# The gated MLP's products and the weighted sums as pairs of 64-row products that change banks halfway, in a sparse attention with a gated MLP

## The chip, the cores and the metric

The kernel runs on one core of a Trainium2 chip. The metric is device time in microseconds (us); lower is better. A profiled execution has a time of its own and a span, the stretch that the profile covers.

## The reference

Inputs are fp32: q, k, v of 4 batches, 8 heads, 768 tokens and 64 dimensions, and the weights of a gated MLP. Attention looks only at the six best of the causal blocks ("chunks") of 32 keys, which are ranked by an upper bound of their scores.

```python
k_min, k_max = min and max of k over each chunk of 32 keys
ub = sum_d maximum(q * k_min, q * k_max)              # bound, causal chunks only
sel = the 6 chunks of highest ub per query
scores = where(sel and key <= query, q @ k.T / 8, -1e9)
x = softmax(scores) @ v                                # heads side by side: [4, 768, 512]
h = relu(x @ w_in)                                     # [4, 768, 1024]
u, v = h[..., :512], h[..., 512:]
v_n = (v - mean(v)) / sqrt(var(v) + 1e-6)
v_s = w_spatial @ v_n + b_spatial                      # mixes tokens
out = (u * v_s) @ w_out                                # [4, 768, 512]
```

## The kernel before

Two heads make a pair `p` (16 in all, four to a batch): their 64 dimensions fill partitions 0 to 63 and 64 to 127. Each pair runs through the same pieces: q, k and v are loaded by SP's queue, cast to fp16 (`cast`), and q and k are turned, by TensorE (`turn`) for pairs 0 to 4 and by a DMA for the others. DVE takes the extremes of each chunk (`ext`, L671). TensorE makes the bounds (`bounds`, L702), DVE finds the sixth best (`top`, `leave`). TensorE makes all causal scores (`pk`, L732, L735 and L786) of which DVE takes the highest per chunk (`mx`, L795 to L807); for the first three pairs (`FOLD = 3`) the scores are first folded in two with a relu on ACT (`fd`, `fr`, `fi`, `fb`, L748 to L766). GpSimd and DVE join both into a bias (`minus`, `kept`, `shift`), TensorE turns it (`turn_bias`, L831). Scores are then made a second time with keys on the partitions, plus the bias (`probs`, L856 and L863), ACT takes exponents (`ex`, L871), GpSimd cuts above the diagonal (`cut`), TensorE makes the weighted sums of v (`weigh`, L885; one piece per head, 21 products of 65 columns), ACT copies them, and GpSimd or DVE normalises (`norm`, L907).

The MLP runs once per batch: `hv` (L937, six pieces of 512 columns), relu (`vr`), mean and variance (`bn`, `rstd`), `vn`; `hu` (L990, eight pieces of 384) with relu (`uT`); `mix` (L1001, eight pieces of six products of 384) is the token mixing; the spatial bias `bB` is added by GpSimd or DVE (`plus`, L1010 and L1012), `gT` (L1019) multiplies by u, and `og` (L1024, six pieces of four products of 512) gives the output, which ACT or DVE copies (`oe`) and SP's queue stores (`od`).

Scores, bounds, `turn_bias` and `fd`/`fb` use products on 64 rows of TensorE: the two heads' products stand next to each other in the program, one on rows 0 to 63, one on 64 to 127, with outputs in different PSUM banks. The weighted sums, the MLP and the turns use all 128 rows. PSUM is divided in three two-bank slots (`two`) for the former and two single banks (`mg`) for the latter; the last batch's MLP uses both.

The order of all pieces is written out: `RANK` gives each piece its rank, `WHERE` the engine where there is a choice, and `Work.order()` runs through time with the cost of each piece (`on`), gives every engine the ready piece of lowest rank, and assigns buffer slots. It reckons 0.095 us where TensorE changes between `TILED` pieces and others:

```python
if e == "PE" and tiled != (name[0] in self.TILED):
    tiled, took = not tiled, took + 0.095
```

The engines then carry out their lists strictly in that order, SP its DMA issues too.

## Time and profile before

| | |
|---|---|
| time, median of 3 runs | 248.54 us (248.27 to 248.81) |
| profiled execution: its own time, its span | 248.22 us, 246.5 us |
| ACT exponents (L871) | 96 instructions, 85.3 us busy |
| DVE peaks (L807) | 104 instructions, 85.3 us busy |
| PE weighted sums (L885) | 672 products, 25.9 us busy |
| PE token mixing (L1001) | 192 products, 30.2 us busy for the 168 in the single banks |
| granted TensorE clock | 1.00 |

A row of the page's list of groups reads: line, engine, operation, output<-inputs, rows*columns of the array or partitions x elements, count | busy time, mean ns of one | idle time just before, and what ended it. PE is TensorE's products, PEld its weight loads, DVE VectorE, ACT ScalarE, POOL GpSimd, SP SyncE. A product's duration reaches from its start until its last result is out, so the products of a run overlap. The profile's timeline gives the start, the length until the last one's end and the count of equal instructions that follow each other.

### The profile page before, as it was taken

The page shows a single profiled execution, that of the slowest core. Times are in us where ns is not written, and L with a number is a line of the kernel's source. Part 1 is how long each engine was busy: PE and PEld are TensorE (multiplying, and loading weights), DVE is VectorE, ACT ScalarE, POOL GpSimd, SP SyncE. Part 2 cuts the span into 40 slices and gives each one's busy share as a digit, 9 for nine tenths or more (in the row PEclk, how much of TensorE's full clock was granted, in tenths as well). Part 3 has the DMA queues.
Part 4 walks back from the last instruction along what each step waited for, and adds up shares of the span by engine and source line. Part 5 has one row for each costly group of instructions (what it writes and reads, how often), then busy time and mean ns, then how long its engine had stood idle before and what let it go on. Part 6 is the DMA issues. An engine that isn't in the chain of part 4 may idle for free.

```text
span 246.5 us, 9019 instructions
## 1 busy us (share of the span) xinstructions
PE 224.9 (91%) x3780; PEld 144.6 (59%) x3780; DVE 206.5 (84%) x512; ACT 191.9 (78%) x298; POOL 165.9 (67%) x209
## 2 busy tenths in 40 slices
PE   0898778878999999999999999999999999999993
PEld 0656457666755675666665576666745566645551
DVE  4799999999999999799998997899998853349670
ACT  3598887979998999587859897897679969767312
POOL 8879749887785377999965929999926147402160
PEclk9999999999999999999999999999999999999999
DMA  7969996699999949484899997128900010350005
GB/s 189 325 186 201 257 242 127 122 164 241 168 186 235 216 82 187 89 170 112 190 161 271 175 200 125 34 75 140 268 22 19 0 36 0 105 188 0 0 28 227
DMA packets 93895, 35.51 MB, mean 144 GB/s; under 512 B 86208, under 2 KB 90144, under 8 KB 93856
## 3 DMA queue, kind: packets, MB, share of 16 engines
q1 hardware_dynamic: 91568, 31.81, 61.9%
q0 software_dynamic: 2016, 2.75, 6.5%
q8 instruction: 29, 0.48, 0.8%
q10 hardware_dynamic: 272, 0.39, 0.5%
q14 instruction: 10, 0.08, 0.1%
HBM read 24.77 MB, written 6.29 MB: 126 GB/s over the span
## 4 chain that ended last, share of the span: by engine, by line
PE 48%; DVE 28%; ACT 14%; DMA 4%; issue 3%; POOL 2%; DVEq 0%; ACTq 0%
DVE cmax L807 11%; PE mg L1001 11%; ACT pr L871 8%; PE mg L1024 6%; PE mg L885 5%; PE two L856 4%; PE mg L937 3%; PE two L863 3%; DVE stats L954 3%; DVE ext L671 3%; PE two L786 3%; DVE top L715 2%; PE mg L990 2%; DMA k<-in_k_dram 2%; DVE cmax L801 2%
## 5 line engine op out<-in xcount | busy, mean ns | idle before, releaser
L871 ACT ACTIVATE pr<-two 128x1024 f16<-128x1024 f32 (+1 forms) x96 | 85.3, 934 | 5.4 <-PE two L863 4.8
L807 DVE TENSOR_REDUCE cmax<-two 128x24 f32<-128x768 f32 (+4 forms) x104 | 85.3, 843 | 3.5 <-PE two L735 2.0
L856 PE MATMUL two<-qT,kT 64*128 64x128 f16 (+3 forms) x384 | 40.5, 258 | 5.4 <-ACT bT L835 1.9
L863 PE MATMUL two<-bT,member 64*128 64x128 f16 (+1 forms) x512 | 39.7, 233 | 0.0
L877 POOL TENSOR_SCALAR_AFFINE_SELECT pr<-pr 128x768 f16<-128x768 f16 x32 | 27.9, 886 | 9.1 <-ACT pr L871 9.0
L1019 POOL TENSOR_TENSOR vr<-tmp,uT 128x384 f16<-128x384 f32 x27 | 24.5, 922 | 11.9 <-DVE tmp L1012 11.8
L671 DVE TENSOR_REDUCE ext<-kT 128x24 f16<-128x768 f16 x32 | 29.5, 936 | 1.9 <-ACT kT L617 1.7
L1001 PE MATMUL mg<-wsT,vn 128*128 128x384 f16 x168 | 30.2, 327 | 0.0
L856 PEld LDWEIGHTS <-kT 64*128 64x128 f16 x384 | 19.9, 94 | 17.2 <-issue 15.1
L863 PEld LDWEIGHTS <-member 64*128 64x128 f16 x512 | 25.7, 94 | 5.1
L885 PE MATMUL mg<-v,pr 128*128 128x65 f16 x672 | 25.9, 194 | 0.7 <-POOL pr L877 0.5
L786 PE MATMUL two<-kT,qT 64*128 64x384 f16 (+4 forms) x182 | 24.6, 280 | 1.4 <-ACT pr L871 0.5
L885 PEld LDWEIGHTS <-pr 128*128 128x128 f16 x672 | 23.1, 98 | 3.6 <-issue 1.0
L1001 PEld LDWEIGHTS <-vn 128*128 128x128 f16 x192 | 17.7, 98 | 12.2 <-issue 0.6
L990 PE MATMUL mg<-xT,w_in_sb 128*128 128x384 f16 x112 | 22.4, 328 | 0.0
L907 POOL TENSOR_TENSOR x<-av,rc 128x768 f16<-128x768 f32 x11 | 16.2, 1469 | 8.8 <-DVE rc L900 4.9
L732 PE MATMUL two<-kT,qT 64*128 64x128 f16 x192 | 19.6, 221 | 2.3 <-ACT qT L617 1.0
L1024 PE MATMUL mg<-w_out_sb,vr 128*128 128x512 f16 x84 | 20.8, 380 | 0.0
L937 PE MATMUL mg<-w_in_sb,xT 128*128 128x512 f16 x84 | 20.3, 380 | 0.4 <-DVE o L619 0.4
L889 ACT COPY av<-mg 128x390 f32<-128x390 f32 x32 | 15.6, 500 | 6.2 <-PE mg L885 6.0
L954 DVE BATCH_NORM_STATS2 stats<-vr 128x6 f32<-128x512 f32 x24 | 16.6, 692 | 4.0 <-ACT vr L942 2.9
L735 PE MATMUL two<-half_ahead,ident 64*128 64x64 f16 x192 | 19.8, 193 | 0.0
(113 smaller groups left out, 496.8 us busy)
## 6 DMA issues: line engine op xcount, KB each, us to landing
q<-in_q_dram SPq DMA_DIRECT2D x16, 384.0 KB, 6.4
v<-in_v_dram SPq DMA_DIRECT2D x16, 384.0 KB, 5.7
out_dram<-o SPq DMA_DIRECT2D x24, 256.0 KB, 2.1
k<-in_k_dram SPq DMA_DIRECT2D x15, 384.0 KB, 5.7
vr<-in_moe_w_spatial_dram POOLq DMA_DIRECT2D x6, 192.0 KB, 5.6
w_in_sb<-in_moe_w_in_dram POOLq DMA_DIRECT2D x4, 256.0 KB, 8.8
w_out_sb<-in_moe_w_out_dram POOLq DMA_DIRECT2D x4, 128.0 KB, 4.5
k<-in_k_dram ACTq DMA_DIRECT2D x1, 384.0 KB, 4.7
```

Of the source, the lines that this page charges most:

```text
L671: nc.vector.tensor_reduce(held["ext", p][:, m], src, axis=AX.X, op=Alu.min if m else Alu.max, negate=(m == 1))
L786: mm(t[:, h, o:o + before], lhsT=qT[rows[h], c], rhs=kT[rows[h], a * CH:a * CH + before], start=True, stop=True)
L807: nc.vector.tensor_reduce(tops(p)[:, i // 2, :, i % 2, a:z], held["two", (p, u)][:, :, o:o + n].rearrange("p h (c e) -> p h c e", e=CH), a ...
L856: mm(t[:, h, z:z + n * P], lhsT=kT[rows[h], keys], rhs=qT[rows[h], i * P:(i + n) * P], start=True, stop=False)
L863: mm(d, lhsT=member[rows[h], r, keys], rhs=bT[rows[h], m * P:(m + w_) * P].rearrange("c (m s) -> c m s", s=P), start=False, stop=(n == 1 o ...
L871: nc.scalar.activation(out=held["pr", p][:, :, c0:c0 + n], in_=held["two", (p, "e", c0)][:, :, 0:n], func=Act.Exp, scale=scale)
L877: nc.gpsimd.affine_select(out=d, in_=d, compare_op=Alu.is_ge, fill=0.0, base=0, channel_multiplier=-1, pattern=[[0, NT], [1, P]])
L885: mm(a[:, i, :], lhsT=pr[:, at[t, i]:at[t, i] + P], rhs=vp[:, h * NT + t, :], start=(t == 0), stop=(t == i))
L937: mm(t, lhsT=held["xT", b][:, ko, i * P:(i + 1) * P], rhs=w_in_sb[:, ko, DH:2 * DH], start=(ko == 0), stop=(ko == NDO - 1))
L990: mm(t, lhsT=w_in_sb[:, ko, db * P:(db + 1) * P], rhs=held["xT", b][:, ko, s * HS:(s + 1) * HS], start=(ko == 0), stop=(ko == NDO - 1))
L1001: mm(t, lhsT=held["vn", b][:, si, db * P:(db + 1) * P], rhs=wsT[:, si, s * HS:(s + 1) * HS], start=(si == 0), stop=(si == NT - 1))
L1024: mm(t, lhsT=held["vr", ("g", b)][:, ko, i * P:(i + 1) * P], rhs=w_out_sb[:, ko, :], start=(ko == 0), stop=(ko == KO - 1))
```

## The change

- `weigh` and the MLP's products of batches 0 to 2 become 64-row pairs. A piece now fills two banks (two heads, two token tiles, or two halves of the columns). In the first round the pair's products use the lower 64 rows for bank 0 and the upper 64 for bank 1, in the second round (`weigh2`, `hv2`, `hu2`, `mix2`, `og2`) the other way round. Between them stands a `relay`: an empty instruction on SP that waits for the first round's last product, and for which the second round's first product waits. There are 58 relays.
- One PSUM ring of four two-bank slots serves everything; evictions of the MLP and of `av` are twice as wide and half as many.
- The spatial bias is added by TensorE: `b_parts` makes two fp16 parts of it, and products with `pick` start each `mix` piece with it. `plus` goes. For batches 2 and 3 DVE's `gT` reads PSUM.
- `FOLD` goes from 3 to 5, other peaks are cut in blocks of 768 and 1024 columns; the causal mask of the bounds is always TensorE's (`EARLY = 16`), so ACT or DVE only copies them.
- The first k comes in two halves; `warm` puts ten products at the start. Casts and `less` may run on ACT, `vn` on GpSimd.
- `RANK` and `WHERE` are new. The last batch's MLP stays on 128 rows.

```diff
-    DELAY = {"PE": 0.25, "DVE": 0.17, "ACT": 0.18, "POOL": 0.14, "SP": 0.0}
-    TILED = ("pk", "probs", "bounds", "turn_bias", "fd", "fb")
+    DELAY = {"PE": 0.25, "DVE": 0.17, "ACT": 0.18, "POOL": 0.14, "SP": 0.15}
+    TILED = ("pk", "probs", "bounds", "turn_bias", "fd", "fb", "weigh", "weigh2", "hv2", "hu2", "mix2", "og2")
+    SPLIT = ("hv", "hu", "mix", "og")
...
-UNITS = [((0, 0, 4), (1, 0, 8)), ((2, 0, 12),), ((3, 0, 16),), ((4, 0, 10),), ((4, 10, 20),), ((5, 0, 12),), ((5, 12, 24),)]
-PEAKS = [(u, i, a, z) for u, segs in enumerate(UNITS) for i, a, z in segs]
+STEPS = ((1, 0, 4), (3, 8, 12), (5, 16, 20))
+UNITS = [STEPS] + [((2 * m, c, c + 8), (2 * m + 1, c, c + 8)) for m, c in ((1, 0), (2, 0), (2, 8))]
+FOLDS = [((4, 0, 16), (5, 0, 16)), ((2, 0, 8), (3, 0, 8)) + STEPS]
+FOLDED = ((0, FOLDS[0]), (1, FOLDS[1][:2]), (1, STEPS))
...
-EARLY = 6
-FOLD = 3
-FOLDS = [(5, 3), (4, 2, 1)]
+EARLY = 16
+FOLD = 5
...
+WARM = (7, 2, 1)
...
-PLUS_POOL = 2
+GATE_POOL = 2
...
-                  cmax=2, kept=2, less=2, av=2, tmp=4, qT=4, rc=2, bias=2, bT=3, kd=2, fr=2, pr=2, x=8, xT=2, vr=1, vn=1, uT=1, o=5, two=3, mg=2))
+                  cmax=2, kept=2, less=2, av=2, tmp=3, qT=4, rc=2, bias=2, bT=3, kd=2, fr=2, pr=2, x=8, xT=2, vr=1, vn=1, uT=1, o=3, two=4))
...
+    for x, n in enumerate(WARM):
+        w.add(("warm", x), {"PE": 0.427 * n}, -9 + 4 * x, after=[(("spark",), ("turn", 0, "k", 1), ("turn", 0, "q"))[x]], new=[("two", ("warm", x))])
...
+            if (p, nm) == (0, "k"):
+                for x in range(2):
+                    add("load", {"SP": 0.46} if x else {"ACT": 0.5}, DUE["load_k"] - 1, nm, x, new=[] if x else [("k32", 0)], old=[("k32", 0)] if x else [], dma=(1.1, 0.4)[x])
+                    add("cast", {"DVE": dve(S // 2, 0.52), "ACT": act(S // 2)}, DUE["cast"], nm, x, after=[("load", 0, nm, x)], new=[] if x else [("k16", 0)],
+                        old=[("k32", 0)] + [("k16", 0)] * x)
+                continue
...
-            add("cast", {"POOL": pool(S)} if p else {"DVE": dve(S, 0.52)} if nm == "k" else {"ACT": act(S)}, DUE["cast"] + 0.05 * (nm == "q"), nm,
+            add("cast", {"POOL": pool(S), "ACT": act(S)} if p else {"DVE": dve(S, 0.52)} if nm == "k" else {"ACT": act(S)}, DUE["cast"] + 0.05 * (nm == "q"), nm,
...
-            add("minus", {"POOL": 0.55}, DUE["leave"] + 0.01, after=[("leave", p)], old=[("bias", p)], new=[("less", p)])
+            add("minus", {"POOL": 0.55, "ACT": 0.35}, DUE["leave"] + 0.01, after=[("leave", p)], old=[("bias", p)], new=[("less", p)])
...
+        at, src = DUE["weigh"], ("two", ("av", p))
+        add("weigh", {"PE": NT * (NT + 1) / 2 * 0.0322}, at, after=[("cut", p, h) for h in range(2) if p >= CUT_PE] + [("cast", p, "v")] + ex,
+            old=[("pr", p), ("v16", p)], new=[src])
+        w.add(("relay", "av", p), {"SP": 0.1}, p + at, after=[("weigh", p)])
+        add("weigh2", {"PE": NT * (NT + 1) / 2 * 0.0322}, at, after=[("relay", "av", p)], old=[("pr", p), ("v16", p), src])
+        add("av", {"ACT": act(2 * NT * (D + 1))}, at, after=[("weigh2", p), ("small",)], old=[src], new=[("av", p)])
+        add("sum", {"DVE": 0.12}, at, after=[("av", p)], old=[("av", p)], new=[("rc", p)])
+        add("inv", {"DVE": 0.14}, at, after=[("sum", p)], old=[("rc", p)])
+        add("norm", {"POOL": 1.5, "DVE": 1.15}, at, after=[("inv", p)], old=[("av", p), ("rc", p)], new=[("x", p)])
...
+        def relay(kind, n, *args):
+            w.add(("relay", kind, b) + args, {"SP": 0.1}, HP * b + DUE["gmlp"] + n * DUE["gmlp_step"], after=[(kind, b) + args])
+
+        def group(n, make, pe, args, need, old, done, on, tag, first):
+            buf = ("two", (make, b) + args)
+            if not last:
+                add(make, {"PE": pe / 2}, n, *args, after=need, old=old, new=[buf])
+                relay(make, n, *args)
+                make += "2"
+                add(make, {"PE": pe / 2}, n, *args, after=[("relay", make[:-1], b) + args], old=old + [buf])
+            else:
+                add(make, {"PE": pe}, n, *args, after=need, old=old, new=[buf])
+            add(done, on, n, *args, after=[(make, b) + args],
+                old=[buf] + ([] if first else [(tag, b)]), new=[(tag, b)] if first else [])
...
-                add("vn", {"ACT": 0.705, "DVE": 0.47} if last else {"ACT": 0.705}, NT + i, i, after=[("rstd2", b, g)], old=[("vr", b)] + ([("vn", b)] if i else []),
+                add("vn", {"ACT": 0.705, "DVE": 0.5} if last else {"ACT": 0.705, "POOL": 0.75}, NT + i, i, after=[("rstd2", b, g)], old=[("vr", b)] + ([("vn", b)] if i else []),
...
+            add("mix", {"PE": (NT + 1) * col(HS)}, NT + 8 + m, *part, after=need, old=[("vn", b)], new=[buf])
+            if not last:
+                relay("mix", NT + 8 + m, *part)
+                add("mix2", {"PE": NT * col(HS)}, NT + 8 + m, *part, after=[("relay", "mix", b) + part], old=[("vn", b), buf])
...
+            if b >= GATE_POOL:
+                add("gT", {"DVE": 0.15 + each * 0.4}, NT + 8 + m, *part, after=[mixed, ("uT", b) + part], old=[buf, ("uT", b)] + [g] * (m > 0), new=[] if m else [g])
+                continue
+            add("ms", {"ACT": act(each * HS)}, NT + 8 + m, *part, after=[mixed], old=[buf], new=[t])
+            for x in range(2):
+                add("gT", {"POOL": 0.92, "DVE": 0.7}, NT + 8 + m, *part, x, after=[("ms", b) + part, ("uT", b) + part],
...
+    def k_b_parts(e, x):
+        if x == 0:
+            nc.gpsimd.tensor_copy(b_row, b_raw)
+            for n, t in enumerate(pick):
+                nc.gpsimd.memset(t, 0.0)
+                for g in range(4 >> n):
+                    nc.gpsimd.memset(t[g * CH:g * CH + 1], 1.0 / (2048.0 if g % 2 else 1.0))
+            return
+        r = slice(D * x - CH, D * x)
+        nc.gpsimd.tensor_sub(b_raw[r], b_raw[r], b_row[r])
+        nc.gpsimd.tensor_scalar(b_row[r], in0=b_raw[r], scalar1=2048.0, scalar2=1.0, op0=Alu.mult, op1=Alu.mult)
...
-            each = [(big, far[:, i])] * (p < EARLY) + [(qT[:, c], x[:, 0]), (qp[:, c], x[:, 0]), (qp[:, c], x[:, 1])]
+            each = [(big, far[:, i])] + [(qT[:, c], x[:, 0]), (qp[:, c], x[:, 0]), (qp[:, c], x[:, 1])] * (i > 0)
...
+    def crossed(key, steps, half):
+        for n in range(len(steps[0])):
+            for x in range(2):
+                o, lhsT, rhs, first, done = steps[x][n]
+                r = slice(D, P) if x != half else slice(0, D)
+                if key[0] == "mix" and half == n == 0:
+                    made = mm(o, lhsT=pick[0][r], rhs=b_row[r, bias_of(key, x)], start=True, stop=False)
+                    first = False
+                made = mm(o, lhsT=lhsT[r], rhs=rhs[r], start=(first and half == 0), stop=(done and half == 1))
+                if half and n == x == 0:
+                    sync(made.ins, held["relay", key])
+        if not half:
+            held["half", key] = made.ins
+
+    def sync(later, earlier):
+        tc.add_manual_dep(later, earlier.name, mybir.DependencyInfo(mybir.DependencyClass.Sync, mybir.DependencyReason.DATA))
+
+    def k_relay(e, *key):
+        held["relay", key] = nc.sync.nop().ins
+        sync(held["relay", key], held["half", key])
...
+    def k_weigh(e, p, half=0):
+        t = held["two", ("av", p)] if half else new("two", ("av", p), [P, 2, 512], F32)
+        vp, pr, o = v16[slot["v16", p]], held["pr", p], t[:, :, 0:NT * (D + 1)].rearrange("p h (i d) -> p h i d", i=NT)
+        crossed(("av", p), [[(o[:, h, i, :], pr[:, h, at[t, i]:at[t, i] + P], vp[:, h * NT + t, :], i == 0, i == NT - 1 and t == i)
+                             for i in range(NT) for t in range(i + 1)] for h in range(2)], half)
...
+    def sums(key, width, count, lhsT, rhs, n, half):
+        t = held["two", key] if half else new("two", key, [P, 2, 512], F32)
+        if key[1] < B - 1:
+            crossed(key, [[(t[:, x, 0:width], lhsT(x, c), rhs(x, c), c == 0, c == n - 1) for c in range(n)] for x in range(count)], half)
             return
+        for x in range(count):
+            if key[0] == "mix":
+                mm(t[:, x, 0:width], lhsT=pick[1], rhs=b_row[:, bias_of(key, x)], start=True, stop=False)
+            for c in range(n):
+                mm(t[:, x, 0:width], lhsT=lhsT(x, c), rhs=rhs(x, c), start=(c == 0 and key[0] != "mix"), stop=(c == n - 1))
...
+    def k_mix(e, b, db, *part, half=0):
+        parts, vn = part or (0, 1), held["vn", b]
+        sums(("mix", b, db) + part, HS, len(parts), lambda n, si: vn[:, si, db * P:(db + 1) * P],
+             lambda n, si: wsT[:, si, parts[n] * HS:(parts[n] + 1) * HS], NT, half)
...
+        if b < GATE_POOL:
+            t = held["tmp", (b, db)][:, part[0]:part[0] + 1]
+        else:
+            t = held["two", ("mix", b, db) + part][:, 0:len(parts), 0:HS]
+        (nc.vector if e == "DVE" else nc.gpsimd).tensor_mul(columns(held["vr", ("g", b)][:, db], parts), t, columns(held["uT", b][:, db], parts))
...
+    for kind in ("weigh", "hv", "hu", "mix", "og"):
+        pieces[kind + "2"] = partial(pieces[kind], half=1)
```

## The prediction

> **What bounds the kernel now.** I read the page first: the engines' shares, then the tenths.
>
> ```profile
> span 246.5 us, 9019 instructions
> ...
> PE 224.9 (91%) x3780; PEld 144.6 (59%) x3780; DVE 206.5 (84%) x512; ACT 191.9 (78%) x298; POOL 165.9 (67%) x209
> ...
> PE   0898778878999999999999999999999999999993
> ...
> DVE  4799999999999999799998997899998853349670
> ```
>
> PE is called busy 91% of the span, but its busy time joins pipelined products, so it says little of full rate. What the tenths show is two regimes: at first DVE is full and PE is not, later PE is full. To find the border I looked in PE's timeline for the first product of the gated MLP (L990, 69.50) and the first of the last batch (L937, 219.15), and asked the stretches between.
>
> ```profile
> 68.98 0.38 PE L856 MATMUL two<-qT,kT 64*128 64x512 f16 x2
> 69.19 0.38 PE L863 MATMUL two<-bT,member 64*128 64x256 f16 x4
> 69.50 0.82 PE L990 MATMUL mg<-xT,w_in_sb 128*128 128x384 f16 x4
> ...
> 209.98 0.27 PE L863 MATMUL two<-bT,member 64*128 64x128 f16 x4
> 210.18 0.84 PE L885 MATMUL mg<-v,pr 128*128 128x65 f16 x21
> ...
> 219.15 0.59 PE L937 MATMUL mg<-w_in_sb,xT 128*128 128x512 f16 x2 [0.45 <-DVE o L619]
> ```
>
> The stretches, columns PE, PEld, DVE, ACT and POOL busy:
>
> ```profile
> 0.00:10.00 10.00, 2.91 (x60) 2.65 (x62) 5.19 (x23) 4.33 (x5) 7.86 (x21) 1.00 0.85 251
> 0.00:69.50 69.50, 54.19 (x1278) 40.33 (x1278) 63.46 (x178) 56.74 (x79) 55.14 (x85) 1.00 0.95 202
> 69.50:219.15 149.65, 147.13 (x2376) 91.86 (x2375) 127.27 (x301) 123.91 (x201) 104.02 (x118) 1.00 0.67 130
> 219.15:246.50 27.35, 23.59 (x128) 12.39 (x127) 15.71 (x34) 11.23 (x20) 6.71 (x7) 1.00 0.20 75
> ```
>
> Stage A (to 69.50, attention alone): DVE is busy 63.46 us, and 4.8 of its 6.0 idle us lie in the first ten. DVE sets it. Stage B (149.65 us, attention beside the MLP of three batches): PE 147.13, DVE and ACT 83 to 85%. PE sets it. Stage C (27.35 us, the last MLP alone): PE again.
>
> **Stage B, what a change of row mode costs.** Products on 64 rows run as pairs on the two halves of the array, those on 128 rows singly, and the old order mixes both.
>
> ```profile
> 153.97 1.15 PE L1001 MATMUL mg<-wsT,vn 128*128 128x384 f16 x6
> 155.06 0.23 PE L856 MATMUL two<-qT,kT 64*128 64x128 f16 x2
> ...
> 155.89 0.25 PE L831 MATMUL two<-ident,bias 64*128 64x64 f16 x6
> 156.08 1.15 PE L1001 MATMUL mg<-wsT,vn 128*128 128x384 f16 x6
> ...
> L1001 PE MATMUL mg<-wsT,vn 128*128 128x384 f16 x168 | 30.2, 327 | 0.0
> ```
>
> Six products of 384 columns take 1.15 us, the last alone 0.327, so one starts each (1.15-0.327)/5 = 0.165 us. A seventh would have started at 153.97+6x0.165 = 154.96; the 64-row pair starts at 155.06, 0.10 late. Back the same way: three pairs of 64 columns at about 0.03 end their stream at 155.98, and L1001 starts at 156.08. Stage B holds 125 such changes in PE's timeline (the first at 69.50 and the last at 210.18 are quoted above, about 0.09 late each). In the new program's order only 5 are left after its first MLP product. Term: 120 x 0.10 = -12.0 us.
>
> **What the pairs cost.** A 128-row product becomes a 64-row pair in each of two rounds, over two outputs. Columns streamed are the same if a pair costs what one 128-row product costs. The pair of 512 columns at 68.98 is followed 0.21 later; 128-row products of 512 take
>
> ```profile
> 237.40 1.03 PE L1024 MATMUL mg<-w_out_sb,vr 128*128 128x512 f16 x4
> ...
> 238.46 0.58 ACT L617 COPY o<-mg 128x512 f32<-128x512 f32 x1 [8.10 <-PE mg L1024]
> ...
> L1024 PE MATMUL mg<-w_out_sb,vr 128*128 128x512 f16 x84 | 20.8, 380 | 0.0
> ```
>
> (1.03-0.38)/3 = 0.217. So the MLP's products change by nothing. For the weighted sums (65 columns) the rows are
>
> ```profile
> 176.38 1.50 PE L885 MATMUL mg<-v,pr 128*128 128x65 f16 x42
> ...
> L885 PE MATMUL mg<-v,pr 128*128 128x65 f16 x672 | 25.9, 194 | 0.7 <-POOL pr L877 0.5
> L831 PE MATMUL two<-ident,bias 64*128 64x64 f16 x96 | 4.2, 192 | 0.6 <-DVE ub L619 0.3 <-DVE cmax L807 0.2
> ```
>
> (1.50-0.194)/41 = 0.032 a product now, and a pair (0.25-0.192)/2 = 0.029 at 155.89: 42 x 0.003 = 0.12 us a pair of heads, twelve in the stage: -1.4 us. The Trainium skill speaks against this: its page "TensorE: Matmul & The Clock Gate" (Wait — 56ns, not 53.3ns?) puts the start-to-start time of matmuls at 25 ns or more however few columns. By it a pair of 65 columns would cost 50 ns, and the sum would be about 14 us higher; the trace disagrees, since six L831 products 25 ns apart would need 0.125+0.192 = 0.32 us, not 0.25.
>
> **The spatial bias by TensorE.** Each two-bank mix piece gets two bias products of 384 columns before its first round. They stand one behind the other on the same half of the array, so that the pieces run one slot out of step: two slots of 0.165 more a piece, 12 pieces, +3.9 us in stage B; in stage C one product a piece, 8 x 0.165 = +1.3 us. What goes is DVE's and POOL's additions (16 each), in engines that stage B and C do not wait for: nothing. The 14 vn moved to POOL have no row there (0.84 us a piece on ACT, 1.23 by L1019's 922 ns for 384); POOL has 45 us to spare in the stage, and attention on PE covers the chain; nothing, or +1 if it shows.
>
> **The relays.** Between the two rounds of each of 58 pieces PE waits for SP, which waited for the first round. The last product of 1.03 us ends 0.17 after its stream and ACT wakes 0.03 later; with two hops I estimate 0.3 to 0.4 us. In the new order most pieces have 0.5 to 1.9 us of other products between their rounds; four have less (none, 0.19, 0.29, 0.32 by columns): 0.8 us in all, half of it in stage A. Take +0.4, and +0.9 for the smaller ring, below.
>
> **Stage B, sum.** The new order enters the MLP with five more exponent blocks, a bounds group, half a weighted sum and part of a head's peaks already done; at 0.21 a 512-column pair and its second product that is 5 x 0.44 + 0.5 + 0.7 + 1.1 = 4.5 us moved to stage A. 149.65 - 12.0 - 1.4 + 3.9 - 4.5 + 1.3 = 137.0 us (133 to 142).
>
> **Stage A.** Here engines other than PE count, and their lists are longer. DVE until the first MLP product: folding for p=3 and p=4 too takes off what the extra head's peaks add, so that the peak reductions stay at about 34 us; one ext, nine maxima, two shifts, two relu of q add: +4 us, 67.5. ACT gets more: six exponent blocks, six casts, four folds' relu, five small copies, less two relu and the merged copies.
>
> ```profile
> L871 ACT ACTIVATE pr<-two 128x1024 f16<-128x1024 f32 (+1 forms) x96 | 85.3, 934 | 5.4 <-PE two L863 4.8
> L617 ACT CAST q<-q 128x768 f16<-128x768 f32 x1 | 0.8, 832 | 2.5 <-DMA q<-in_q_dram 2.5
> L753 ACT ACTIVATE fr<-two 128x896 f16<-128x896 f32 (+1 forms) x6 | 5.7, 972 | 0.9 <-PE two L748 0.9
> ```
>
> Back to back they run 0.12 us denser than their means: 6 x 0.92 + 6 x 0.71 + 4 x 0.86 + 2.5 = 15.7 us on top of 53 (what the old list's 79 instructions need back to back; they were spread over 56.74 us): 68.7. Both lists thus need 67.5 to 69 us, ACT from about 4 us on, DVE from about 5. The start gains:
>
> ```profile
> 6.14 0.82 PE L652 MATMUL mg<-ident,k 128*128 128x128 f16 x6 [6.14 <-DVE k L619]
> 70.17 0.50 PE L609 MATMUL mg<-ident,vr 128*128 128x128 f16 x6
> ```
>
> half of k is loaded and cast first (its load ends 5.5 us in), and six transposes at the start take 0.82 us against 0.50 later, which the ten warming products, in PE time idle until 6.14, may mend: -1 us. At best 72.5, with DVE and ACT waiting for each other up to 80; I take 76.0, about 95% of either, as DVE now.
>
> **Sum.** 76.0 + 137.0 + (27.35 + 1.3) = 241.6 us span. The profiled execution took 248.22 with a span of 246.5, 1.7 more; it lies 0.3 under the median of 248.54. Forecast: 243.3 us.
>
> **Rivals.** (1) The ring: three two-bank slots and two single banks become four two-bank slots that hold transposes and MLP pieces as well. A single output lives from 237.40 to 239.04 now; a two-round piece of 512 columns at least 0.87+0.5+0.87+0.2+1.0 = 3.5 us. Estimated so, stage B needs 18 x 3.5 (v and output products) + 12 x 2.9 (u) + 12 x 3.7 (mix) + 12 x 2.8 (weighted sums) + 61 x 1.7 (exponents) + 54 x 1.6 (peaks) + 20 x 1.0 = 386 us of slots, over four 97 of its 137 us; each 0.1 us that these 190 pieces wait in DVE's or ACT's queue adds 190 x 0.1 / 4 = 4.8. From a mean wait of 0.85 us the ring sets the stage; at 1.0, +7 us: 250. The Trainium skill, "TensorEngine Tiling (Array Packing)" (Gotcha 1: PSUM Pressure), warns that row tiling raises PSUM pressure; no row of the old kernel shows four slots. (2) The other side: SP's queue. 33 of 58 relays stand right behind a DMA issue on SP.
>
> ```profile
> SPq L929 <- DVE x L907: 13.0, 1, 13.0
> SPq L929 <- POOL x L907: 10.0, 2, 6.0
> ```
>
> SP stands up to 13 us on a transpose's input today, and nobody cares; with a relay behind it PE, in order, would stand too, and every stage behind. It decides from 5.3 us of lateness in all; ten relays late by 1.2 us, +12: 255. For it: the waits above; against: the order issues SP's steps only when its plan has their inputs. (3) The pairs don't overlap as said, and each small pair costs 50 ns: 257; against it stands the L831 row.
>
> **Chances.** Forecast 0.72, ring 0.13, SP's queue 0.13, pairs 0.02. The forecast's bounds are 72.5+133+28.2 and 80+142+29 with 1.7 each, 235.4 to 252.7, mostly under 248. Faster by over 0.2% (0.5 us, about what a measurement here can tell): 0.74, with a little of the ring; within it 0.04; slower 0.22. Range 235.5 to 252.0: it takes in the ring and leaves most of SP's case and the pairs out.
>
> **What would show it.** Right: the timeline with about 48 changes of row mode, pairs of 512 columns 0.21 apart in both rounds, the first MLP product at 73 to 80 us with ACT over 90% busy before it, stage B near 137 us, and SP releasing PE in under 1 us in all. Wrong: waits of PE for SP in the list of waits, waits of PE for ACT and DVE evictions of several us in stage B (the ring), a first MLP product after 82 us, or pairs of 65 columns over 0.04 us.

## The result

The changed kernel takes 270.47 us, median of four runs (268.43 to 271.98), beside 248.41 (247.76 to 248.81) for the kernel before: ratio 1.089 (95% interval 1.080 to 1.097). It is 22 us slower, where 5 us faster was forecast. The profiled run took 271.55 us with a span of 269.8.

The page of the changed kernel: span, busy time, and the tenths of PE, DVE and the granted clock.

```profile
span 269.8 us, 11396 instructions
...
PE 231.9 (86%) x5006; PEld 162.9 (60%) x5006; DVE 201.8 (75%) x469; ACT 192.2 (71%) x259; POOL 143.2 (53%) x189
...
PE   6688876769959869975999699999999999999994
...
DVE  6699938357958976998699799978976853448652
...
PEclk9899978886988999999899999999999999999999
```

Two rows have changed their kind. DVE, whose row before stood at 9 from the third to the 16th slice and at 7 or more up to the 32nd, has holes. And TensorE's clock, which the row of the old kernel shows granted in full throughout, is not:

```profile
PEclk9999999999999999999999999999999999999999
```

The three stages of the changed kernel (to the first MLP product at 91.9, to the first one of the last batch at 241.1, to the end; columns PE, PEld, DVE, ACT and POOL busy, then the mean granted clock):

```profile
0.00:91.90 91.90, 70.47 (x1722) 50.57 (x1723) 67.62 (x180) 71.20 (x98) 63.92 (x99) 0.89 0.94 175
91.90:241.10 149.20, 136.48 (x3152) 99.13 (x3147) 118.49 (x257) 110.89 (x145) 77.56 (x89) 0.99 0.62 113
241.10:269.80 28.70, 24.95 (x138) 13.22 (x136) 15.66 (x34) 10.10 (x17) 1.74 (x2) 1.00 0.26 96
```

Stage C is what was forecast (28.70 for 28.65). Stage A takes 91.9 for 76.0 and stage B 149.2 for 137.0. DVE and ACT have the work that was forecast for stage A (67.62 and 71.20 us busy, for 67.5 and 68.7): the lists are right, but neither engine is full.

Where PE's time went I worked out from the start of every product in the trace. "Stream" is the columns at 0.213 us per 512; "half clock" what the stretches at half clock add to it; "no cause" gaps ahead of an instruction that waits for no semaphore; "waits" the other gaps over 0.15 us; then the gaps at changes of row mode, and the rest. (The first product starts at 6.1 us before the change and at 1.5 after it.)

```
                      length  stream  half clock  waits  no cause  mode changes  rest
before, stage A         69.5    35.8         0.0   16.2       0.0           4.2   7.2
before, stage B        149.7   124.3         0.0    5.2       0.0          12.2   8.3
changed, stage A        91.9    44.7         8.4   25.0       5.4           3.1   3.8
changed, stage B       149.2   121.4         1.7   13.2       5.0           0.4   7.6
```

In stage B the mode changes went as forecast (12.2 to 0.4) and the stream fell by 2.9. What ate it: waits (+8.0), gaps without a cause (+5.0), which the old kernel does not have, and half clock (+1.7).

**The gaps without a cause.** The timeline of PE in the middle of such a gap (idle time and releaser in brackets; lines of other pieces left out):

```profile
123.08 0.84 PE L959 MATMUL two<-v,pr 64*128 64x65 f16 x42 [0.72 <-ACT pr L938]
...
124.66 0.19 PE L775 MATMUL two<-ext,qT 64*128 64x24 f16 x2
124.68 0.17 PE L775 MATMUL two<-ext,qp 64*128 64x24 f16 x1
127.17 0.20 PE L775 MATMUL two<-ext,qp 64*128 64x24 f16 x3 [2.31 <-issue]
127.22 0.18 PE L775 MATMUL two<-far,big 64*128 64x24 f16 x2
```

PE stops for 2.31 us inside a group of products that have all their inputs. Counted from 0 in order of time, all of PE's instructions in the trace together (loads, products and 19 others), the product at 127.17 is number 4801, which is 193 more than a multiple of 256. The same holds for the load or product after each of the other five such gaps (ending at 59.65, 77.97, 88.82, 150.01 and 170.37; with this one 10.4 us in the table). It holds for 42 of the 46 such gaps over 0.15 us in the experiments below too; the other four, of 0.2 to 0.3 us, lie near 112 to 115 us in e9, e12, e15 and e16. The DMA queues say what that is:

```profile
q8 instruction: 29, 0.48, 0.8%
```

That is the row of the kernel before; the changed one has

```profile
q8 instruction: 39, 0.64, 1.1%
```

0.48 and 0.64 MB are PE's 7560 and 10012 loads and products at about 64 bytes: queue 8 carries PE's instructions, in blocks of 16 KB, 256 each. The DMA records give each block's time. A block's transfer begins when PE has entered the block before it (1.06 us later in the median before, 1.59 in the changed kernel between 10 and 180 us, at most 4.5), lasts 0.9 to 1.6 us, and its first instruction never ran less than 1.2 us after its end. From these figures I estimate that a block must last PE some 3 to 6 us. In the kernel before every block was there 2.0 us or more before it was used; in the changed kernel nine of 38 were used less than 1.7 us after they landed, and six held PE up; these I call late blocks. By the rows a round of weighted sums is now 42 products and as many loads in 0.67 us (to the next piece), 256 instructions in 2.0 us, where the single products took 4.1.

The Trainium skill, "Runtime: NRT & Kernel Launch" (Instruction fetch mechanics), states refills in blocks of 16 KiB or 256 instructions, which the trace bears out. Of what PE holds it gives 128 KiB in one sentence and two blocks in another; the trace fits two, since a block's transfer waits until PE has entered the block before it. It calls the cost of crossing into a new one "mostly hidden", which these rows do not.

**The clock.** Four slices of 5 us in the changed kernel:

```profile
30.00:35.00 5.00, 2.94 (x95) 2.19 (x94) 4.48 (x28) 4.69 (x9) 4.79 (x5) 0.99 0.42 87
35.00:40.00 5.00, 4.13 (x101) 3.10 (x102) 1.18 (x2) 1.99 (x3) 5.00 (x8) 0.67 1.14 150
40.00:45.00 5.00, 2.73 (x56) 1.82 (x56) 5.00 (x10) 2.68 (x4) 3.69 (x6) 1.00 1.10 209
45.00:50.00 5.00, 3.79 (x43) 2.31 (x40) 1.53 (x4) 4.24 (x5) 3.63 (x5) 0.66 0.66 133
```

The clock is either full or half, in windows of 3.41 us; seven windows of this run are at half, 23.9 us. Six of them follow windows in which the products, by their columns, filled 0.16 to 0.35 of the time, the seventh one at half clock; the thinnest windows that were not so followed had 0.39, 0.42 and 0.43. After 10 us the kernel before has none under 0.42. Three of the six thin windows hold a late block. The Trainium skill, "TensorE: Matmul & The Clock Gate" (Part 1: The HAM clock gate), states the two rates and the window of 3413 ns, and the trace agrees; it names an idle window as what lowers the clock, and here windows busy for a third did.

**Waits.** From PE's list:

```profile
PE two L775 <- issue: 4.3, 3, 2.3
PE two L852 <- issue: 3.0, 1, 3.0
PE two L959 <- SPq L969: 3.0, 3, 1.8
```

The third row is the relays. To split the other waits I took, for every gap over 0.15 us, the last reader of the tile that had the same banks before, and the last writer of its inputs; the one that ended 0.05 us before the product is the cause. Waiting for the ring came to 17.0 us in stage A from 10 us on and 8.4 in stage B, 13.3 and 3.7 in the kernel before.

### The profile page after: what moved, and what is told of

Same layout as the page of the kernel before. It is cut to its first block, busy times and chain, and to the rows that moved or that the text cites. A ratio compares the mean times of both kernels' runs of the same rounds, so it can differ in the third digit from the quotient of the medians.

```text
span 269.8 us, 11396 instructions
## 1 busy us (share of the span) xinstructions
PE 231.9 (86%) x5006; PEld 162.9 (60%) x5006; DVE 201.8 (75%) x469; ACT 192.2 (71%) x259; POOL 143.2 (53%) x189
## 2 busy tenths in 40 slices
DMA packets 94034, 35.69 MB, mean 132 GB/s; under 512 B 86080, under 2 KB 90272, under 8 KB 93984
## 4 chain that ended last, share of the span: by engine, by line
PE 55%; DVE 18%; ACT 9%; POOL 6%; issue 6%; DMA 3%; SPq 1%; POOLq 0%; DVEq 0%; ACTq 0%
PE two L959 26%; DVE cmax L872 9%; PE two L987 9%; PE two L923 5%; PE two L930 4%; ACT pr L938 4%; DMA q<-in_q_dram 3%; DVE ext L744 3%; PE two L775 2%; PE two L852 2%; DVE stats L1042 1%; POOL b_raw L650 1%; DVE top L788 1%; PE two L665 1%; DVE bias L797 1%
## 5 line engine op out<-in xcount | busy, mean ns | idle before, releaser
L872 DVE TENSOR_REDUCE cmax<-two 128x24 f32<-128x768 f32 (+3 forms) x91 | 91.7, 1022 | 23.4 <-PE two L852 10.2
L959 PE MATMUL two<-v,pr 64*128 64x65 f16 x1344 | 28.6, 195 | 4.7 <-issue 1.7
L959 PEld LDWEIGHTS <-pr 64*128 64x128 f16 x1344 | 26.4, 97 | 7.5 <-issue 3.4
L959 PE MATMUL two<-wsT,vn 64*128 64x384 f16 x288 | 27.3, 322 | 0.0
L959 PE MATMUL two<-xT,w_in_sb 64*128 64x384 f16 x192 | 18.4, 323 | 2.8 <-SPq L969 2.7
L852 PE MATMUL two<-kT,qT 64*128 64x256 f16 (+1 forms) x198 | 16.8, 254 | 3.9 <-issue 3.0
L959 PEld LDWEIGHTS <-vn 64*128 64x128 f16 x288 | 15.4, 94 | 6.7 <-issue 0.8
L884 POOL TENSOR_TENSOR kept<-less,cmax 128x288 f32<-128x288 f32 x16 | 12.9, 811 | 12.3 <-DVE cmax L872 10.0
L959 PE MATMUL two<-w_in_sb,xT 64*128 64x512 f16 x144 | 18.0, 376 | 0.0
L959 PE MATMUL two<-w_out_sb,vr 64*128 64x512 f16 x144 | 17.3, 376 | 0.5 <-DVE cmax L872 0.5
L990 ACT COPY av<-two 128x780 f32<-128x780 f32 x16 | 13.0, 814 | 5.9 <-PE two L959 5.7
```

Of the source, the lines that this page charges most:

```text
L852: mm(o, lhsT=qT[r, c], rhs=kT[r, x.start * CH:x.stop * CH], start=True, stop=True)
L872: nc.vector.tensor_reduce(x, t[:, :, o:o + n].rearrange("p h (m c e) -> p h m c e", m=m, e=e), axis=AX.X, op=Alu.max)
L959: made = mm(o, lhsT=lhsT[r], rhs=rhs[r], start=(first and half == 0), stop=(done and half == 1))
L990: nc.scalar.copy(av[slot["av", p]][:, :, :, 0:D + 1], held["two", ("av", p)][:, :, 0:NT * (D + 1)].rearrange("p h (i d) -> p h i d", i=NT))
```

## The experiments

All are edits of the changed kernel but the last; the ratio is to runs of the kernel before on the same chip. T: late blocks, with the clock behind them. R1: order and ring. C: the half clock has a cost of its own. P: POOL's preparation of the bias. "First" is the first MLP product, "B" from there to the first product of the last batch, both of the profiled run.

```
kernel                            median us   ratio to before (95%)    first       B
changed kernel                       270.47   1.089 (1.080 to 1.097)    91.9   149.2
e1_single_all                        283.84   1.141 (1.134 to 1.148)    88.1   164.7
e2_single_av                         267.54   1.075 (1.068 to 1.082)    88.0   150.3
e3_fill                              268.42   1.076 (1.069 to 1.083)    91.3   150.7
e4_light                             259.54   1.042 (1.037 to 1.048)    87.0   140.3
e5_parts_late                        275.17   1.111 (1.106 to 1.116)    91.9   152.6
e6_light_late                        267.50   1.077 (1.072 to 1.083)    88.8   148.9
e7_light_late_fill                   270.31   1.090 (1.085 to 1.096)    91.7   149.9
e8_single_av_late                    273.32   1.101 (1.096 to 1.106)    87.8   155.5
e9_light_gapfill                     258.96   1.042 (1.037 to 1.048)    87.0   140.6
e10_gapfill                          266.02   1.068 (1.061 to 1.075)    92.1   146.2
e11_single_av_gapfill                268.08   1.076 (1.071 to 1.081)    90.4   148.6
e12_light_gapfill_parts              257.33   1.035 (1.030 to 1.039)    84.2   141.7
e13_gapfill_parts                    263.07   1.058 (1.053 to 1.063)    87.7   144.9
e14_single_gapfill_parts             265.04   1.065 (1.059 to 1.070)    88.2   148.8
e15_light_gapfill_kept               257.99   1.038 (1.031 to 1.045)    87.1   141.2
e16_light_gapfill_kept_parts         257.00   1.035 (1.030 to 1.040)    84.0   141.1
e18_before_light (kernel before)     248.22   0.998 (0.996 to 1.000)    69.8   149.7
```

The stage times of e3 and e10 come from runs 4.0 and 2.7 us over their medians. None is faster than the kernel before; of the changed ones with all their loads e13 is the shortest.

**e1 and e2: pairs undone.**

```diff
 def crossed(key, steps, half):
+    if True:                      # e2: if key[0] == "av"
+        for x in range(2) if not half else ():
+            if key[0] == "mix":
+                mm(steps[x][0][0], lhsT=pick[1], rhs=b_row[:, bias_of(key, x)], start=True, stop=False)
+            for o, lhsT, rhs, first, done in steps[x]:
+                held["half", key] = mm(o, lhsT=lhsT, rhs=rhs, start=(first and key[0] != "mix"), stop=done).ins
+        return
```

> The pairs alone are undone: every sum of the weighed values and of the first three batches' MLP is formed by single 128-row products at the place of the first half, the second half is empty; order, ring, relays and the bias by TensorE stay. 3950 products for 5006, so 31 instruction blocks for 39; by the order 130 changes of row mode for 48 (82 x 0.10 us = +8.2 us). Theory T (late instruction blocks cost 8.5 us by themselves, and they and other gaps put the clock to half in 24 us): late blocks gone (-8), three of the half-clock windows gone (-4), +8: 266 us (262 to 269). Rival R1 (the order and the one ring cost the time, the pairs nothing): only the mode changes are added, 278 us, the half-clock time is as long as before.

283.84: neither theory. The gaps without a cause are gone, as T says (0.6 us in stage A, none in B, for 5.4 and 5.0), and first comes 3.8 us earlier. But stage B takes 164.7, of which 27.5 are waits of PE, 25.7 of them for the ring, and 6.2 mode changes.

```profile
88.10:252.80 164.70, 146.04 (x2305) 92.50 (x2304) 118.58 (x254) 108.66 (x144) 77.86 (x89) 1.00 0.52 100
```

The order was laid out for two rounds apart; with all the work in the first round evictions bunch and PE waits for them. In this order the undoing of the pairs costs 13 us; what pairs gain or lose by themselves e1 doesn't show, since it also moves the second round's work forward.

> The pairs are undone for the weighed sums alone (672 products fewer, 34 instruction blocks for 39, 76 mode changes for 48: +2.8 us). Theory T: the late blocks fall from 8.5 us to about 3, one or two half-clock windows go: 264 to 268 us. Rival R1: 273 us.

267.54, inside T's range and far from R1's 273: the gaps at block borders fall from 10.4 to 2.4 us with 672 products fewer, and that pays for 28 more mode changes (2.2 us in stage B) and 2.7 us more of waits there. What is left, 2.9 us less than the changed kernel, is at the edge of the noise: the two intervals just overlap.

**e3: fillers.**

```diff
-WARM = (7, 2, 1)
+WARM = (7, 2, 6)
+FILL = {("weigh", 0): 5, ("bounds", 3): 2, ("probs", 1, 0): 4, ("fi", 4, 1): 2, ("bounds", 4): 1}
...
```

> Products of a constant tile are added where PE waits in stage A (5 single ones ahead of the third turn of q, 5, 2, 4, 2 and 1 pairs ahead of five pieces between 31 and 57 us), 4 us of products in all, overwritten by what follows them. Theory T: those windows are no longer thin, so the half-clock windows that follow them (near 11, 35, 45 and 59 us) go, those after late blocks (near 79 and 127 us) stay: about 264 us (261 to 268), half clock 24 us -> 10 or less. Rival R1 (the clock follows the waiting and costs nothing of its own): 270 to 273 us.

268.42, between the two. The windows only moved: half clock near 12, 43 (two), 101 and 132 us. It settles nothing, also because a filler at the head of a piece waits for that piece's banks, and the added products let the planner's order shift (see e15).

**e4: the loads made light.**

```diff
 t = held[nm + "32", p] if x else new(nm + "32", p, o, F32)
+# ahead of it, where an earlier pair had the same buffer and layout ("last"):
+held[nm + "32", p] = held[nm + "32", last]
+nc.sync.dma_start(out=held[nm + "32", p][0:1], in_=src[0:1])
+return
```

> The loads of q, k and v that could reuse a buffer of the same layout move one partition for 128 (the old data are computed on again); PE, SP and all queues keep their instructions. It takes most of the data traffic away from the instruction blocks. Theory T: blocks start within about 1 us after PE enters the block before, late blocks 8.5 -> 2 us or less, the half-clock windows after them go: 258 to 262 us. Rival R1: 268 to 272 us. Rival R2 (SP's queue of loads and relays holds the kernel): 268 to 272 us as well, as SP's order and waits are the same.

259.54, as T says, 10.9 us less with the same instructions on PE. Bytes fall from 35.69 to 20.86 MB. A block's transfer now begins 0.83 us after the entry in the median (1.59), and the gaps at block borders fall from 10.4 to 2.7 us. The relays gain too:

```profile
PE two L857 <- issue: 1.8, 1, 1.8
...
PE two L964 <- SPq L974: 0.3, 1, 0.3
```

The relays' 3.0 us become 0.3, so e4 does not part blocks from relays; the trace puts them at 7.7 and 2.7 us. The loads' own lateness falls too: by the lists of waits POOL and ACT wait 4.0 and 1.8 us for loads of v and q in the changed kernel, 1.1 and 0.7 in e4. Whether that counts in the new order no run parts from the blocks; but e2, with all its loads, loses most of its block gaps too. The stages:

```profile
0.00:87.00 87.00, 68.71 (x1724) 49.09 (x1725) 68.67 (x183) 70.85 (x98) 63.73 (x99) 0.92 0.59 104
87.00:227.30 140.30, 134.43 (x3150) 97.46 (x3147) 117.67 (x254) 110.05 (x145) 77.75 (x89) 1.00 0.35 64
```

With the blocks in time stage B is 140.3, inside the 133 to 142 of the prediction. Stage A is 11 us over its 76.0.

**e18, the control for e4.** The same edit in the kernel before.

> The kernel before with the light loads of e4 (old data computed on again), as the control for e4. Theory T (in the old kernel every instruction block arrives at least 2 us before it is needed, so the data traffic costs PE nothing): 246.5 to 248.5 us. Rival D (the loads cost both kernels time by themselves, and e4's 11 us say nothing of the change): 238 to 244 us.

248.22 beside 248.87 of the runs on that chip: the old kernel gains 0.65 us, so nearly all of the 11 us of e4 belongs to the change. Its stages:

```profile
0.00:69.80 69.80, 53.65 (x1279) 40.33 (x1280) 63.76 (x178) 56.56 (x80) 55.06 (x86) 1.00 0.60 117
69.80:219.50 149.70, 147.24 (x2377) 91.76 (x2376) 127.69 (x301) 123.81 (x201) 103.71 (x117) 1.00 0.35 70
```

**e5 to e8: POOL's preparation moved, first place.** Between 21.8 and 32.3 us POOL prepares the bias, which the prediction never costed, and then cuts the first weights (lines of other work left out):

```profile
21.84 0.84 POOL L643 CAST b_row<-b_raw 128x768 f16<-128x768 f32 x1
22.61 0.22 POOL L645 MEMSET pick<- 128x128 f16 x1
22.88 0.90 POOL L647 MEMSET pick<- 1x128 f16 x4
23.84 0.21 POOL L645 MEMSET pick<- 128x128 f16 x1
24.11 0.43 POOL L647 MEMSET pick<- 1x128 f16 x2
...
25.35 1.64 POOL L650 TENSOR_TENSOR b_raw<-b_raw,b_row 32x768 f32<-32x768 f32 x1
27.08 0.83 POOL L651 TENSOR_SCALAR b_row<-b_raw 32x768 f16<-32x768 f32 x1
...
29.76 1.64 POOL L650 TENSOR_TENSOR b_raw<-b_raw,b_row 32x768 f32<-32x768 f32 x1
31.49 0.83 POOL L651 TENSOR_SCALAR b_row<-b_raw 32x768 f16<-32x768 f32 x1
...
33.05 2.10 POOL L944 TENSOR_SCALAR_AFFINE_SELECT pr<-pr 128x768 f16<-128x768 f16 x2
```

```diff
 order, slot = work.order()
+parts = [x for x in order if x[0][0] == "b_parts"]
+order = [x for x in order if x[0][0] != "b_parts"]
+n = [x[0] for x in order].index(("rstd1", 0, 0))
+order[n:n] = parts
```

e5 is this alone, e6 this and e4, e8 this and e2; e7 is e6 with

```diff
-WARM = (7, 2, 1)
+WARM = (7, 2, 6)
+# behind each turn of the chunk bias, p < 8: 6 pairs of 320 columns of spark into t[:, g, 192:512]
```

> POOL's preparation of the spatial bias (a cast, two subtractions, two scalings, eight memsets: 7.5 us between 21.8 and 32.3 us of the changed kernel, after which POOL cuts the first weights that PE waits for) is moved in POOL's order to just ahead of the first batch's rstd, where POOL waits 14 us anyway; nothing else changes. Theory P (that preparation, uncosted in the prediction, is on the path of stage A: PE waits 1.3 us for the cut, the thin window is followed by a half-clock one, DVE and ACT stand behind both): first MLP product 3 to 5 us earlier, 265 to 268 us. Rival T alone (blocks and clock only): 269 to 271 us.

> The light loads of e4 and POOL's preparation moved as in e5 (old data computed on again). Theory P: 254 to 257 us, first MLP product at 82 to 84 us for 87.0. Rival (POOL is not on the path): 259 to 260 us as e4.

> e6 with products of a constant tile where PE is thin in stage A: 6 warming products for 1 ahead of the third turn, and 6 pairs of 320 columns behind each of the first eight turns of the chunk bias, into columns nobody reads (7.5 us of products in all). Theory C (the half clock costs about what it takes from PE in stage A, 5.6 us in e4): half-clock time below 5 us in all, and 2 to 4 us faster than e6 in spite of the added products. Rival (the clock follows the waiting and costs little): as e6 or up to 4 us slower.

> The weighed sums as single products (e2) and POOL's preparation moved (e5), with all loads as they are: 262 to 265 us by T and P together; 267 us if POOL is not on the path.

All four missed what P and C gave: e5, e6 and e8 came out 5 to 8 us slower than the kernels they build on. The place was bad. From the first hv of the first batch to its first mix e5 needs 36.9 us for 31.1, since rstd stood behind the preparation; PE's waits in stage B went from 13.2 to 19.0. In stage A first did not move (91.9 for 91.9, 88.8 for 87.0), but the clock was half for more windows (four in a row from 33.7 us in e6), so these runs cannot speak on P. e7's fillers cost 3 us, which is inside its rival's range, but four windows in stage A stayed at half, so it does not test C.

**e9 to e11: fillers only in gaps.** They go into unread columns of tiles that are held anyway:

```diff
-WARM = (7, 2, 1)
+WARM = (7, 2, 6)
+FILL = {("turn_bias", 1): 7, ("probs", 1, 2560): 5, ("turn_bias", 3): 3, ("turn_bias", 4): 3,
+        ("probs", 7, 2560): 4, ("turn_bias", 8): 2, ("fd", 3, 1): 18}
+def fill(name, t, a):             # called at the end of the piece
+    for n in range(FILL.get(name, 0)):
+        for h in range(2):
+            r = slice(h * D, (h + 1) * D)
+            mm(t[:, h, a:512], lhsT=spark[r, 0:P], rhs=spark[r, 0:512 - a], start=True, stop=True)
```

e9 is this on e4, e10 on the changed kernel, e11 on e2.

> The light loads of e4, and products of a constant tile only where PE stood idle in the traces of e4 and of the changed kernel, written into columns nobody reads of a tile that is held anyway, so that they wait for no buffer: 5 more warming products ahead of the third turn, 1.0 us ahead of the first weighed sums, 0.9, 0.8, 0.4, 0.4 us ahead of gaps near 41, 48, 54 and 71 us, 0.9 us near 123 us. Theory C (half-clock windows that follow thin ones are on the path of stage A): half clock 16 -> 5 us or less and 254 to 257 us. Rival (the clock costs little; buffers and order hold stage A): 259 to 261 us.

> The changed kernel with the same fillers and all its loads. Theory C: half clock 24 -> 12 us or less (windows behind late blocks may stay), 264 to 267 us. Rival: 269 to 271 us.

> Single products for the weighed sums (e2) and the same fillers, all loads: the shortest correct form that the runs so far point to short of the old order. Theories T and C: 262 to 265 us, half clock below 6 us. Rival (clock of no account): 267 us as e2.

e9 has the clock at 0.993, one window at half for four, and is no faster: 258.96 for 259.54, first at 87.0 for 87.0. That speaks against C in stage A; but the fillers put 4.4 us more products there (48.7 us by their columns for 44.3), so they can hide a gain of that size. e10 came out at 266.02, 4.5 us under the changed kernel, as C had it, but with the same stage A (92.1 for 91.9), although half clock there takes 2.9 for 8.4 us and late blocks 5.9 for 5.4. As far as its profiled run shows the gain (2.8 us of the span), it is in stage B, where late blocks are 2.1 for 5.0 us. e11, for which C and T gave 262 to 265, gained nothing on e2.

What e9 shows of stage A is in DVE's list of waits:

```profile
DVE ext L757 <- ACT kT L681: 5.5, 1, 5.5
DVE cmax L886 <- POOL kept L898: 4.2, 1, 4.2
```

The second: a pair's first peaks wait for its buffer, which POOL's sum kept still reads, queued behind the preparation.

**e12 to e14: the preparation in POOL's idle gaps.**

```diff
 # parts taken out of the order as in e5
+for x, at in zip(parts, (("kept", 7), ("minus", 8), ("minus", 8))):
+    order.insert([y[0] for y in order].index(at), x)
```

> e9 (light loads, fillers) with POOL's preparation of the spatial bias moved into POOL's idle gaps of 3.2 and 4.4 us at 91 and 96 us (a part ahead of the sum kept of pair 7, two ahead of the next pair's minus). Theory P (the preparation, 7.5 us that the prediction did not cost, holds stage A): DVE's wait of 4.15 us near 34 us goes, first MLP product at 81 to 84 us for 87.0, 253 to 256 us for 259.0. Rival R (the four-slot ring and the order hold stage A): first MLP product at 86 to 87 us, 258 to 260 us.

> The same with all loads as the changed kernel has them (e10 with the preparation moved). Theory P: 261 to 264 us for 266.0. Rival R: 265 to 267 us.

> e11 (single products for the weighed sums, fillers, all loads) with the preparation moved. Theory P: 262 to 265 us for 268.1. Rival R: 267 to 269 us.

P holds for stage A: the wait of 4.2 us is gone from DVE's list, and first comes 2.8 us earlier in e12 (84.2), 4.4 in e13, 2.2 in e14. The times fall by 1.6, 3.0 and 3.0 us, less than P gave in e12 (257.33, between the two ranges), as P gave in e13 (263.07) and at the edge of its range in e14 (265.04).

**e15 and e16: the order exactly kept.** As e9 and e12, with the planner's durations for the warming products left at (7, 2, 1).

> In e3, e7 and e9 to e14 the five added warming products also entered the planner's durations, so 14 of 403 PE pieces of the order moved by up to ten places. Here e9 with every engine's order exactly that of e4: light loads, fillers, nothing moved. Theory C (the half clock costs what it takes from PE): 254 to 257 us, first MLP product at 83 to 85 us. Rival (the clock only shows that PE waits): as e4, 258 to 260 us, first MLP product at 86 to 88 us, with half clock 5 us or less for 16.

> e15 with POOL's preparation of the spatial bias in POOL's idle gaps (as e12). Theory P: 2 to 4 us faster than e15, first MLP product 2 to 4 us earlier. Rival R (ring and order): within 1 us of e15.

e15: 257.99, first at 87.1, with the clock at 0.992. That is the rival's stage A again and not C's 83 to 85, with the same reservation on the fillers; over the whole kernel 1.5 us less than e4 lies within the two intervals. e16: first 3.1 us earlier, as P says; but the time is only 1.0 us less, which is R's figure, half of P's least, and within the two intervals (the two profiled runs, at 258.94 and 255.82 us, are 3.1 apart).

```profile
0.00:84.00 84.00, 68.82 (x1801) 49.30 (x1803) 71.14 (x182) 70.73 (x98) 56.07 (x86) 1.00 0.59 108
84.00:225.10 141.10, 135.19 (x3161) 98.07 (x3159) 118.70 (x255) 110.07 (x145) 85.12 (x102) 1.00 0.32 64
```

**What is left.** In e16 most of the late blocks, the relays' lateness, the half clock and the preparation are out of the way, and it is still 12.5 us over the span forecast: 8.0 in stage A, 4.1 in B. In stage A DVE and ACT are busy 85% and 84% of the time. DVE's 71.1 us are 3.6 more than the forecast's 67.5, and its idle time is 12.9 us, where 76.0 left 8.5; one wait of 3.4 us is for a late turn of k (5.5 in e9), and moving that ahead was not tried. PE waits 19.0 us for the ring in A and 9.3 in B (13.3 and 3.7 in the kernel before). The profile's own releasers, which count only from the end of the product before, give 7.9 and 4.1 us for 7.1 and 0.8, so the ring shows clearly in B alone. That the smaller ring and the order hold the rest is what the trace suggests; no run shows it.

## Why the prediction was wrong

The span came out 28.2 us over the 241.6 of the sum: 15.9 in stage A, 12.2 in stage B, nothing in C.

- **Mode changes, right.** 48 of them, stage B's from 12.2 to 0.4 us, for -12.0 forecast.
- **Pairs of MLP products, right.** From the timeline of PE,

```profile
156.33 1.89 PE L959 MATMUL two<-w_out_sb,vr 64*128 64x512 f16 x16
```

eight pairs, the last product lasting 0.376: (1.89-0.376)/7 = 0.216 us a pair of 512 columns, for 0.21.
- **Weighted sums, mis-sized.** A pair of 65 columns is 0.032 us (21 pairs in 0.84 at 123.08, the last product lasting 0.195), not 0.029: nothing gained, for -1.4. The rival by which small pairs cost 50 ns is out.
- **Bias on TensorE, mis-sized and half forgotten.** The two bias products lie on the two halves of the array (`crossed` gives them different rows), not on the same one, and take one slot as a pair, not two:

```profile
133.01 0.34 PE L957 MATMUL two<-b_row,pick 64*128 64x384 f16 x2
133.17 1.15 PE L959 MATMUL two<-wsT,vn 64*128 64x384 f16 x12
134.15 0.24 PE L805 MATMUL two<-kT,qT 64*128 64x128 f16 x2
```

0.16 us from the bias pair to the next, and the twelve others in 0.98: 12 x 0.16 = 1.9 us, for 3.9. But its preparation, 7.5 us of POOL in stage A, was not in the sum: I counted what the step adds on PE and what it takes from DVE and POOL, not what it brings them. It costs stage A 2 to 4 us (e12 to e16), the kernel 1 to 3.
- **Relays: +0.4 forecast, 3.0 measured,** three of them (0.9, 1.8 and 0.3 us at 95.0, 100.6 and 177.6 us): SP was issuing transposes from 91.44 to 94.88, 95.72 to 100.51 and 175.40 to 177.53 us, with the relay behind them. The rival of SP's queue was right in kind; its 12 us were four times too much.
- **The step that failed first: the cost of an instruction.** The sum took products by their columns. Two products for one also means twice the instructions in the same time, and these have to come in. No part of the prediction looked at that; no rival did. It is 10.4 us of gaps on PE, and with the relays about 10.9 us of the kernel's time (e4, e18). Without it stage B falls into the forecast's range (140.3 us in e4), helped a little by terms that cancel: the bias 2.0 us under its forecast, the weighted sums 1.4 over.
- **The step that failed next: stage A at 95% of either list.** The lists were right to 3 us, the filling was not. The 95% counts from when each engine starts; of the whole 76.0 us it is 89% for DVE and 90% for ACT. Measured are 74% and 77%, and 85% and 84% in e16. In the kernel before only DVE was that full (91%); ACT was busy 56.74 of 69.50 us, 82%. Giving ACT 14 us more and calling both full had no row behind it.
- **The ring.** The rival put it into stage B, at +7 us, with a chance of 0.13. In B it is +4.7 us of waits for +0.9 forecast. In A it may be part of the 8 us that are left in e16; that stays open.

Of the signs named beforehand, two for "right" came, the 48 changes of row mode and the pairs of 512 columns 0.216 apart. Those for "wrong" came too: a first MLP product after 82 us, PE waiting for SP, and for evictions in stage B; pairs of 65 columns stayed under 0.04 us. None of them named the largest loss; "issue" in the list of waits did.

## What to carry to other kernels

Count instructions as well as columns: ask how long 256 of PE's instructions last at the densest place, and compare that with the 3 to 6 us that a block needed here, by the estimate above, while loads were running; PE idle "<-issue" inside a group whose inputs are there is the sign. A step moved to another engine brings its preparation along, on a queue that may be full just then: cost it at the place where it stands. Do not take two engines that feed each other as full at once unless a row shows it; take the fill that the profile has.

## What the runs showed of the hardware

- PE's instructions come through a DMA queue of their own, 256 at a time, the next block only after the one before it has been entered; with loads running, blocks used up faster stopped PE for up to 3.0 us.
- In the changed kernel products filling 0.16 to 0.35 of a 3.41 us window were followed by half clock, windows of 0.39 to 0.43 were not. The border is not sharp: a window of 0.34 was not followed by it in e3, one of 0.37 was in e15. At half clock, where 0.5 is all that fits, the clock can stay down (behind a window of 0.38 at 58.8 us in the changed kernel, behind three of 0.30 to 0.36 from 33.7 us in e6). Yet taking nearly all of it away with fillers in e9 and e15 gained nothing in stage A: no run shows that the low clock cost that stage time, though the fillers' own 4.4 us may hide some.
- Two products of 65 columns on the two halves of the array take 0.032 us as a pair (21 pairs in 0.84 us, the last product lasting 0.195), with loads of their own.
